# Moving work between engines and along the queues of two gated units: slope products, a normalisation and a gradient product

## The chip, the cores and the metric

The kernel runs on one core of one Trainium2 chip. Its time is the device time of a run in microseconds (us); a lower time is better. The time before is the median of six runs. All busy times, waits and durations come from one profiled execution of the kernel before. In the profile PE is TensorE (PEld its weight loads), DVE is VectorE, ACT is ScalarE, POOL is GpSimd, and SP is SyncE, which here only issues DMAs.

## The reference

Two kinds of layer alternate, A, B, A, B, over a residual x of 2048 rows and 512 columns, and the kernel returns the output and the gradients with respect to x and all weights.

```
def A(x): q, k, v = split(x @ wqkv)              # 32 heads of 16
          phi = t -> where(t > 0, t + 1, exp(t)) + 1e-6
          kv, z = phi(k)^T v, sum(phi(k));  return (phi(q) kv / (phi(q) z + 1e-6)) @ wo
def B(x): g = x @ w_gate;  u = x @ w_up;  h = sigmoid(g) * u;  return h @ w_down
x = x + A(layernorm(x));  x = x + B(layernorm(x))
x = x + A(layernorm(x));  x = x + B(layernorm(x))
out, vjp = jax.vjp(f, x, wqkv, wo, w_gate, w_up, w_down);  grads = vjp(grad_out)
```

The change lies in the two B layers, the gated units (GLU), with w_gate and w_up of 512 by 1376 and w_down of 1376 by 512. For the gradient a GLU needs, beside h, the two slopes: that of h with respect to u, which is sigmoid(g), and that with respect to g, which is sigmoid(g) (1 - sigmoid(g)) u.

## The kernel before, in words

The 2048 rows are 16 tiles of 128 and are worked on in 4 blocks of 4 tiles (512 rows). The 1376 inner columns of a GLU are 11 chunks of 128 (the last one overlaps its neighbour). Layers are numbered 0 to 3; 1 and 3 are the GLUs. The forward pass runs over the four layers, then the backward pass over layers 2, 1 and 0 (the backward products of layer 3 that lead to its input are made inside its forward loop), and the weight gradients come last.

**One chunk of a GLU** (`glu`). TensorE makes g (4 matmuls into one PSUM bank) and u (4 into another). ScalarE turns g in place into t = tanh(-g/2) (L647) and makes 1 - t in bf16 (L648). VectorE multiplies it by u/2: that is h (`hh`, L649). ScalarE makes 1 + t (L650), and GpSimd multiplies it by h (L651). So `sd` holds twice both slopes side by side. The forward pools have 8 PSUM banks, all under one tag, so a matmul group waits until an older bank has been read for the last time: u's by L649, g's by L650.

**The first GLU** (`b_fwd`, layer 1). For each block: the down product of the block before (44 matmuls into 4 banks, L675), its 4 residual adds on VectorE (`add_x`, L428), the normalisation of these 4 tiles for layer 2 (`nxt.need`), then the 11 chunks. The stores of a chunk's `hh` and `sd` (L657, L668) go to SP's queue one chunk later. Between the chunks the caller advances the second half of layer 0 by a step (`A0.second`): queries are evicted and scaled (L534, L535, L546), y products made and added, and these tiles normalised for layer 1. In the last block the keys of layer 2 are made between chunks 4, 6, 8 and 10.

**The normalisation** (`LN.one`, layers 1 to 3) takes two tiles at once: ScalarE makes the negative mean (L296) and twice the squared deviations with their sum (L299), GpSimd makes rstd (L301, L302), VectorE applies it (L304, two operations), and SP issues a transposing DMA (L307). After the fourth tile GpSimd's queue stores the block (L310).

**The last GLU** (`b_both`, layer 3). Per chunk it calls `glu`, then makes the gradient of h (4 matmuls), which ScalarE halves into `dhh` (L732, two buffers), and VectorE multiplies both slopes by it in place (L733): that is `dd`. SP stores it (block 0, L781) or transposes it into a staging tile (later blocks, L763), which is flushed at the second chunk of the next group. GpSimd's queue stores `hh`. After chunk 1 of a block come the down product of the block before (into the output, L718) and the 88 matmuls from its `dd` to the gradient of the normalised input (L790), with the backward normalisation (L855 to L862). Block 0 runs beside the second half of layer 2; when that is done, the transposed weights for the backward pass are loaded (L418, L419), held by `k.last_mul`, the last product L733 issued, and GpSimd clears their overlap (L420).

**What sets the order.** Each engine works its own queue in order. The order within a queue is set when the program is built, by the place in the code and a priority (`high_priority`), and it can differ from the order of the code; `after` pins some pairs by hand. Semaphores hold data dependences across engines.

Of the kernel before, what the change touches and what calls it, by code (L numbers as in the profile page):

```python
# [9 lines left out]
ACT = mybir.ActivationFunctionType  # L10
ALU = mybir.AluOpType
# [9 lines left out]
P = 128  # L21
NST = S // P
# [6 lines left out]
NB = 4  # L29
NBLK = NST // NB  # L30
SB = NB * P
# [7 lines left out]
def rows(st, n=1):  # L39
    return slice(st * P, (st + n) * P)  # L40


def by_tile(ap2d, st, n):
    return ap2d[rows(st, n), :].rearrange("(n p) d -> p n d", p=P)
# [133 lines left out]
def mm4(k, out, lhs, rhs, n=NDC):  # L178
    for c in range(n):
        i = k.nc.tensor.matmul(out, lhsT=lhs(c), rhs=rhs(c), start=(c == 0), stop=(c == n - 1))  # L180
    return i
# [153 lines left out]
def forward(k):  # L335
    nc, tc = k.nc, k.tc
    with ExitStack() as ctx:
# [22 lines left out]
        for b, fc in b_fwd(k, 1, lns[1], lns[2]):  # L360
            if fc < 7:
                next(second, None)
            if b == NBLK - 1 and fc in (4, 6, 8, 10):
                A2.keys((fc - 4) // 2)
# [58 lines left out]
def add_x(k, st, y_ps, x=None):  # L423

    if st % 2 == 0:
        k.sums[st // 2] = k.small.tile([P, 2], F32, name="x_sum", bufs=NST)
    t = k.sums[st // 2][:, st % 2:st % 2 + 1]
    k.nc.vector.scalar_tensor_tensor(k.xs[st][:], y_ps[:], 1.0, k.xs[st][:] if x is None else x, ALU.mult, ALU.add,  # L428
                                     accum_out=t)
# [202 lines left out]
                yield True  # L632


def glu(k, hT, fc):

    nc = k.nc
    g_ps = k.ps.tile([P, SB], F32, name="g_ps", tag="bank")
    mm4(k, g_ps[:], lambda c: k.wg[:, c, FC0[fc]:FC0[fc] + P], lambda c: hT[:, :, c, :])
    u_ps = k.ps.tile([P, SB], F32, name="u_ps", tag="bank")  # L640
    mm4(k, u_ps[:], lambda c: k.wu[:, c, FC0[fc]:FC0[fc] + P], lambda c: hT[:, :, c, :])
    hh = k.p_hh.tile([P, SB], BF16, name="hh_t")
    if k.n_sd % 2 == 0:
        k.sd2 = k.p_sd.tile([P, 2, 2, SB], BF16, name="sd_t", tag="sd")
    sd = k.sd2[:, k.n_sd % 2]
    k.n_sd += 1
    nc.scalar.activation(g_ps[:], g_ps[:], ACT.Tanh, scale=-0.5)  # L647
    nc.scalar.activation(sd[:, 0, :], g_ps[:], ACT.Identity, bias=k.onef[:], scale=-1.0)  # L648
    nc.vector.scalar_tensor_tensor(hh[:], sd[:, 0, :], 0.5, u_ps[:], ALU.mult, ALU.mult)  # L649
    nc.scalar.activation(sd[:, 1, :], g_ps[:], ACT.Identity, bias=k.onef[:])  # L650
    nc.gpsimd.tensor_tensor(sd[:, 1, :], sd[:, 1, :], hh[:], ALU.mult)  # L651
    return hh, sd


def store_hh(k, sv, b, fc, hh, eng):
    p0, f1 = (FDUP if fc == NFC - 1 else 0), min((fc + 1) * P, F)
    eng.dma_start(out=sv["hhT"][fc * P:f1, b * SB:(b + 1) * SB], in_=hh[p0:P])  # L657


def b_fwd(k, l, ln, nxt):  # L660
    nc, sv = k.nc, k.sv[l]
    hhs, late = {}, []

    def store():

        b, fc, hh, sd = late.pop()
        store_hh(k, sv, b, fc, hh, nc.sync)
        nc.sync.dma_start(out=sv["sd"][b, fc], in_=sd.rearrange("p a b -> p (a b)"))  # L668

    def down(b):  # L670
        ys = [k.ps.tile([P, D], F32, name="y_ps", tag="bank") for _ in range(NB)]
        for fcs in (range(NFC - 1), (NFC - 1,)):
            for j in range(NB):
                for fc in fcs:
                    nc.tensor.matmul(ys[j][:], lhsT=hhs[b][fc][:, rows(j)], rhs=k.wd[:, fc, :],  # L675
                                     start=(fc == 0), stop=(fc == NFC - 1))
        for j in range(NB):
            add_x(k, b * NB + j, ys[j])
        nxt.need(b * NB + NB - 1)

    for b in range(NBLK):
        hhs[b] = []
        if b:
            down(b - 1)
        for fc in range(NFC):
            hh, sd = glu(k, ln.hT[b], fc)
            hhs[b].append(hh)
            if late:
                store()
            late.append((b, fc, hh, sd))  # L690
            yield b, fc
    store()
    down(NBLK - 1)


def last_grads(k, b):

    k.gns[b] = k.p_h.tile([P, NB, D], BF16, name="gn_t", tag="h_t")
    k.nc.sync.dma_start(out=k.gns[b][:], in_=by_tile(k.g_in, b * NB, NB))
    k.gTs[b] = k.p_hT.tile([P, NDC, SB], BF16, name="gT3_t", tag="hT_t")  # L700
    k.nc.sync.dma_start_transpose(out=k.gTs[b][:], in_=k.g_in[rows(b * NB, NB), :])


def b_both(k, l, ln, ctx):

    nc, sv = k.nc, k.sv[l]
    pool = lambda name, bufs: ctx.enter_context(k.tc.tile_pool(name=name, bufs=bufs))
    hhs, dds, gns, gTs = {}, {}, k.gns, k.gTs
    k.n_t, k.fused = 2, lambda st: True

    def down(b):
        for j in range(NB):
            st = b * NB + j
            y_ps = k.ps.tile([P, D], F32, name="y_ps", tag="bank")
            mm4(k, y_ps[:], lambda fc: hhs[b][fc][:, rows(j)], lambda fc: k.wd[:, fc, :], NFC)
            if j % 2 == 0:
                ost = k.p_o.tile([P, 2, D], BF16, name="o0_t")
            nc.vector.tensor_tensor(ost[:, j % 2, :], y_ps[:], k.xs[st][:], ALU.add)  # L718
            if j % 2:
                k.st.dma_start(out=by_tile(k.out0, st - 1, 2), in_=ost[:])  # L720

    for b in range(NBLK):
        ln.need(b * NB + NB - 1)
        hhs[b], dds[b] = [], []
        if b == 1:
            k.p_ln, k.p_o, k.p_nat = pool("ln3", 2), pool("o3", 2), pool("nat", 2)
        for fc in range(NFC):
            hh, dd = glu(k, ln.hT[b], fc)
            ps = k.ps.tile([P, SB], F32, name="dhh_ps", tag="bank")
            mm4(k, ps[:], lambda c: k.wdT[:, c, FC0[fc]:FC0[fc] + P], lambda c: gTs[b][:, c, :])  # L730
            dhh = k.p_dhh.tile([P, SB], BF16, name="dhh_t")
            nc.scalar.mul(dhh[:], ps[:], 0.5)  # L732
            k.last_mul = nc.vector.tensor_tensor(dd, dhh[:].unsqueeze(1).to_broadcast([P, 2, SB]), dd, ALU.mult)  # L733
            hhs[b].append(hh)
            dds[b].append(dd)
            if b:
                turn_dd(k, sv, b, fc, dd)
            else:
                store_dd(k, sv, b, fc, dd, nc.sync)
            store_hh(k, sv, b, fc, hh, k.st)  # L740
            if fc == 1 and b:
                down(b - 1)
                dh_b(k, l, b - 1, dds[b - 1], ln.h[b - 1], gns[b - 1])
            if fc == 3 and b + 1 < NBLK:
                last_grads(k, b + 1)
                if b:
                    ln.need((b + 2) * NB - 1)
            if b == NBLK - 1 and fc == 5:
                k.early = a_grads(k, 0)
            yield b, fc  # L750
    b = NBLK - 1
    down(b)
    dh_b(k, l, b, dds[b], ln.h[b], gns[b])
    flush_nat(k)


def turn_dd(k, sv, b, fc, dd):

    i, f = divmod(fc, 4)
    p0 = FDUP if fc == NFC - 1 else 0  # L760
    if f == 0:
        k.nat = k.p_nat.tile([P, 2, NB, D], BF16, name="nat_t")
    k.nc.sync.dma_start_transpose(  # L763
        out=k.nat[:, :, :, f * P - p0:(f + 1) * P - p0].rearrange("p a j f -> p (a j) f"),
        in_=dd.rearrange("p a s -> p (a s)"))
    if f == 1:
        flush_nat(k)
    if f == 3 or fc == NFC - 1:
        w = SETS[i][1]
        k.nats.append((sv["ddN"][b, i, :, :, :, 0:w], k.nat[:, :, :, 0:w]))  # L770


def flush_nat(k):
    while k.nats:
        dst, t = k.nats.pop()
        k.nc.sync.dma_start(out=dst, in_=t)


def store_dd(k, sv, b, fc, dd, eng):
    p0, f1 = (FDUP if fc == NFC - 1 else 0), min((fc + 1) * P, F)  # L780
    eng.dma_start(out=sv["ddT"][:, fc * P:f1, b * SB:(b + 1) * SB].rearrange("a p s -> p a s"), in_=dd[p0:P])  # L781


def dh_b(k, l, b, dds, h, up=None):
    for j in range(NB):
        st = b * NB + j
        dh_ps = k.ps.tile([P, D], F32, name="dh_ps", tag="bank")
        for i in range(2 * NFC):
            a, fc = divmod(i, NFC)
            k.nc.tensor.matmul(dh_ps[:], lhsT=dds[fc][:, a, rows(j)], rhs=(k.wuT, k.wgT)[a][:, fc, :],  # L790
                               start=(i == 0), stop=(i == 2 * NFC - 1))
        ln_bwd(k, l, st, dh_ps[:], h[:, j, :], k.xs[st][:] if up is None else up[:, j, :])
# [462 lines left out]
```

## Time and profile before

| what | value |
|---|---|
| runs before, median (lowest to highest) | 1134.0 us (1131.3 to 1139.45) |
| profiled execution: run, span | 1132.12 us, 1130.3 us |
| granted TensorE clock | 0.995 of full speed |
| first GLU, from its first to its last matmul | 77.2 to 213.7 us |
| last GLU | 267.5 to 523 us |
| ScalarE busy in the chunks of block 1 of the first GLU (110.5 to 136.0) | 23.07 of 25.5 us |
| VectorE, GpSimd busy in the same stretch | 18.18, 15.65 us |
| TensorE busy in block 0 of the last GLU (267 to 324) | 48.49 of 57 us |
| L648, L650 on ScalarE, mean of one | 690 ns, 688 ns |
| L647, L732 on ScalarE, median of one | 593 ns, 597 ns |
| matmul of 512 columns, median record | 379 ns |

A group's line reads: line, engine, operation, output and inputs, shape, count, busy time and mean of one, then the engine's idle time just before these instructions and what ended most of it. In the timeline a row is start, duration, engine, line, operation, and in brackets the idle time before it and its releaser; xN says how many instructions are merged. In the waits a row is the waiting instruction, what it waited for, total time, how often, and the longest.

### The profile page before, as it was taken

The numbers are of one execution on the slowest core, as the hardware profiler recorded it, in microseconds if no ns is written. First come the engines' busy times: TensorE is split into PE (matmuls) and PEld (weight loads), VectorE is DVE, ScalarE is ACT, GpSimd is POOL, SyncE is SP. The second block draws the span as 40 slices with busy tenths as digits, with TensorE's granted clock in tenths as the row PEclk, the third lists the DMA queues.
The fourth block names the chain that finished last, engine by engine and source line by source line (L and its number), as shares of the span: only waits on it lengthen the run. The fifth ranks groups of instructions, "written<-read, shape, count | busy, mean of one in ns | idle before, by whom it ended". The sixth has DMA issues, their size and how long they took to land.

```text
span 1130.3 us, 15573 instructions
## 1 busy us (share of the span) xinstructions
PE 1073.6 (95%) x5529; PEld 508.8 (45%) x5624; DVE 527.5 (47%) x983; ACT 487.8 (43%) x1002; POOL 327.0 (29%) x427
## 2 busy tenths in 40 slices
PE   6989999998889999999998999999899999999998
PEld 3444444444344444444443444444444444465443
DVE  7685655667734445434756624556666200000100
ACT  3476977547635556453433533335336200000011
POOL 5425755303632526141533200003523100001110
PEclk9999999999999999999999999999999999999999
DMA  9987988679994939399995798759972797699995
GB/s 263 263 230 241 255 242 248 187 181 236 291 228 88 255 78 248 77 259 269 235 336 154 218 273 231 241 171 301 317 233 81 172 280 172 146 185 253 274 234 133
DMA packets 376557, 248.12 MB, mean 220 GB/s; under 512 B 288784, under 2 KB 341040, under 8 KB 374688
## 3 DMA queue, kind: packets, MB, share of 16 engines
q1 hardware_dynamic: 361424, 197.73, 70.1%
q0 software_dynamic: 15056, 49.39, 12.8%
q8 instruction: 44, 0.72, 0.3%
q14 instruction: 33, 0.27, 0.1%
HBM read 74.48 MB, written 102.20 MB: 156 GB/s over the span
## 4 chain that ended last, share of the span: by engine, by line
PE 27%; issue 20%; POOL 3%; DMA 3%; DVE 2%; ACT 1%; SPq 0%; POOLq 0%; DVEq 0%; ACTq 0%
PE dh_ps L885 7%; PE dhh_ps L180 3%; PE fill_ps L236 3%; PE dw_ps L1199 2%; PE CT_ps L972 2%; PE dq_ps L180 2%; PE dh_ps L790 2%; PE dh_ps L1107 2%; PE dh_ps L1046 1%; DMA qr_l<-sv_qr 1%; POOL out_dram L1127 1%; PE dpk_ps L180 1%; POOL x L865 1%; PE y_ps L180 1%; DMA hf_t<-sv_hhT 1%
## 5 line engine op out<-in xcount | busy, mean ns | idle before, releaser
L1199 PE MATMUL dw_ps<-set_t,h_all 128*128 128x512 bf16 (+1 forms) x1008 | 203.9, 362 | 2.3 <-ACT dw_new L1126 1.5
L1199 PEld LDWEIGHTS <-h_all 128*128 128x128 bf16 x1024 | 100.0, 98 | 105.6 <-issue 2.1
L651 POOL TENSOR_TENSOR sd_t<-sd_t,hh_t 128x512 bf16<-128x512 bf16 x88 | 107.8, 1235 | 119.8 <-DVE hh_t L649 89.2
L1126 ACT CAST dw_new<-dw_ps 128x512 bf16<-128x512 f32 (+1 forms) x40 | 19.9, 572 | 219.0 <-PE dw_ps L1199 155.2
L855 ACT ACTIVATE t_sb<-dh_ps,rstd 128x512 f32<-128x512 f32 x64 | 43.5, 680 | 134.1 <-PE dh_ps L790 81.6
L180 PE MATMUL g_ps<-hT_t,wg 128*128 128x512 bf16 x352 | 90.5, 379 | 7.3 <-DVE hh_t L649 4.0
L1223 DVE TENSOR_TENSOR dw_new<-dw_ps,part_l 128x512 bf16<-128x512 f32 (+1 forms) x11 | 7.3, 687 | 179.7 <-PE dw_ps L1217 166.2
L180 PE MATMUL u_ps<-hT_t,wu 128*128 128x512 bf16 x352 | 90.5, 379 | 0.6 <-DVE hh_t L649 0.6
L180 PE MATMUL dhh_ps<-gT_t,wdT 128*128 128x512 bf16 x341 | 89.3, 379 | 0.5
L649 DVE SCALAR_TENSOR_TENSOR hh_t<-sd_t,u_ps 128x512 bf16<-128x512 bf16 x88 | 59.3, 679 | 14.1 <-ACT sd_t L648 13.5
L885 PE MATMUL dh_ps<-wuT,dd_t 128*128 128x512 bf16 x173 | 65.6, 379 | 0.2
L885 PE MATMUL dh_ps<-wgT,dd_t 128*128 128x512 bf16 x170 | 64.5, 379 | 0.2
L1127 POOL DMA_DIRECT2D out_dram<-dw_new x36 | 19.2, 541 | 151.1 <-ACT dw_new L1126 149.6
L648 ACT ACTIVATE sd_t<-g_ps,onef 128x512 bf16<-128x512 f32 x88 | 60.8, 690 | 2.5
L650 ACT ACTIVATE sd_t<-g_ps,onef 128x512 bf16<-128x512 f32 x88 | 60.6, 688 | 0.0
L733 DVE TENSOR_TENSOR sd_t<-dhh_t,sd_t 128x1024 bf16<-128x1024 bf16 x44 | 30.4, 692 | 61.5 <-POOL sd_t L651 60.2
L908 DVE TENSOR_TENSOR dd_t<-dhh_t,sh_t 128x1024 bf16<-128x1024 bf16 x44 | 29.9, 689 | 58.6 <-ACT dhh_t L906 45.0
L647 ACT ACTIVATE g_ps<-g_ps 128x512 f32<-128x512 f32 x88 | 52.4, 602 | 8.8 <-PE g_ps L180 8.7
L180 PEld LDWEIGHTS <-wg 128*128 128x128 bf16 x352 | 33.9, 98 | 47.1 <-issue 8.8
L180 PEld LDWEIGHTS <-wu 128*128 128x128 bf16 x352 | 34.4, 98 | 42.4 <-issue 0.9
L790 PEld LDWEIGHTS <-sd_t 128*128 128x128 bf16 x352 | 34.4, 98 | 41.6
L885 PEld LDWEIGHTS <-dd_t 128*128 128x128 bf16 x352 | 34.4, 98 | 41.6
(172 smaller groups left out, 1854.7 us busy)
## 6 DMA issues: line engine op xcount, KB each, us to landing
sv_sd<-sd_t SPq DMA_DIRECT2D x44, 256.0 KB, 2.9
sv_ddT<-dd_t SPq DMA_DIRECT2D x40, 256.0 KB, 4.2
sv_h<-h_t POOLq DMA_DIRECT2D x16, 512.0 KB, 5.6
sv_qr<-pe_t POOLq DMA_DIRECT2D x16, 512.0 KB, 5.2
qr_l<-sv_qr SPq DMA_DIRECT2D x8, 1024.0 KB, 7.4
sh_t<-sv_sd SPq DMA_DIRECT2D x8, 1024.0 KB, 7.1
h_all<-sv_h SPq DMA_DIRECT2D x16, 512.0 KB, 5.8
sv_ddN<-nat_t SPq DMA_DIRECT2D x6, 1024.0 KB, 4.4
```

The costliest lines, as they stand in the source:

```text
L180: i = k.nc.tensor.matmul(out, lhsT=lhs(c), rhs=rhs(c), start=(c == 0), stop=(c == n - 1))
L236: nc.tensor.matmul(ps[0:w, :], lhsT=t[:, st, 0:w], rhs=self.g[st // NB][:, st % NB, :], start=(st == 0), stop=(st == NST - 1))
L647: nc.scalar.activation(g_ps[:], g_ps[:], ACT.Tanh, scale=-0.5)
L648: nc.scalar.activation(sd[:, 0, :], g_ps[:], ACT.Identity, bias=k.onef[:], scale=-1.0)
L649: nc.vector.scalar_tensor_tensor(hh[:], sd[:, 0, :], 0.5, u_ps[:], ALU.mult, ALU.mult)
L650: nc.scalar.activation(sd[:, 1, :], g_ps[:], ACT.Identity, bias=k.onef[:])
L651: nc.gpsimd.tensor_tensor(sd[:, 1, :], sd[:, 1, :], hh[:], ALU.mult)
L790: k.nc.tensor.matmul(dh_ps[:], lhsT=dds[fc][:, a, rows(j)], rhs=(k.wuT, k.wgT)[a][:, fc, :], start=(i == 0), stop=(i == 2 * NFC - 1))
L855: nc.scalar.activation(t_sb[:], dh_ps, ACT.Identity, scale=rstd, accum_out=c1[:])
L885: nc.tensor.matmul(acc[b][j][:], lhsT=dd[:, a, rows(j)], rhs=(k.wuT, k.wgT)[a][:, fc, :], start=(fc == 0 and a == 0), stop=(fc == NFC - 1 ...
L1127: (eng or k.st).dma_start(out=k.outs[nm][rs, cs], in_=new[0:r, 0:w])
L1199: k.nc.tensor.matmul(ps[ic][:, 0:w], lhsT=h_m[:, ic * P:(ic + 1) * P], rhs=t_m, start=(m == 0), stop=(m == n - 1))
```

## The change

`glu` gets a flag `fused`. With it, the second slope is made by one VectorE operation, (t + 1) times h, which reads t from PSUM, instead of the ScalarE and the GpSimd operation. The first GLU sets it in its odd chunks (1, 3, 5, 7, 9); the last GLU does not. In the first GLU the normalisation of the block before moves from its place after the residual adds to two places behind chunks 2 and 4, two tiles each; the last block's stays behind its adds. In the last GLU the product L733, and with it the store or transposes of `dd`, is issued one chunk later, behind the `dhh` of the next chunk; the last chunk's follows the loop.

```
-def glu(k, hT, fc):
+def glu(k, hT, fc, fused=False):
...
-    nc.scalar.activation(sd[:, 1, :], g_ps[:], ACT.Identity, bias=k.onef[:])
-    nc.gpsimd.tensor_tensor(sd[:, 1, :], sd[:, 1, :], hh[:], ALU.mult)
+    if fused:
+        nc.vector.scalar_tensor_tensor(sd[:, 1, :], g_ps[:], 1.0, hh[:], ALU.add, ALU.mult)
+    else:
+        nc.scalar.activation(sd[:, 1, :], g_ps[:], ACT.Identity, bias=k.onef[:])
+        nc.gpsimd.tensor_tensor(sd[:, 1, :], sd[:, 1, :], hh[:], ALU.mult)
...
         for j in range(NB):
             add_x(k, b * NB + j, ys[j])
-        nxt.need(b * NB + NB - 1)
...
         for fc in range(NFC):
-            hh, sd = glu(k, ln.hT[b], fc)
+            hh, sd = glu(k, ln.hT[b], fc, fc % 2 == 1)
...
             late.append((b, fc, hh, sd))
+            if b and fc in (2, 4):
+                nxt.need((b - 1) * NB + (1 if fc == 2 else 3))
             yield b, fc
     store()
     down(NBLK - 1)
+    nxt.need(NST - 1)
...
+    def scale(b, fc, dhh, dd):
+        k.last_mul = nc.vector.tensor_tensor(dd, dhh[:].unsqueeze(1).to_broadcast([P, 2, SB]), dd, ALU.mult)
+        if b:
+            turn_dd(k, sv, b, fc, dd)
+        else:
+            store_dd(k, sv, b, fc, dd, nc.sync)
+
+    late = []
...
             nc.scalar.mul(dhh[:], ps[:], 0.5)
-            k.last_mul = nc.vector.tensor_tensor(dd, dhh[:].unsqueeze(1).to_broadcast([P, 2, SB]), dd, ALU.mult)
+            if late:
+                scale(*late.pop())
+            late.append((b, fc, dhh, dd))
             hhs[b].append(hh)
             dds[b].append(dd)
-            if b:
-                turn_dd(k, sv, b, fc, dd)
-            else:
-                store_dd(k, sv, b, fc, dd, nc.sync)
...
+    scale(*late.pop())
     b = NBLK - 1
     down(b)
```

## The prediction

> **What bounds the kernel now.** I read the page first, then TensorE's waits over both gated units, then busy times by stretch, then the timeline around each stall. All times are us of the profiled execution: span 1130.3, run 1132.12, so 1.82 lies around the span; the median of the runs is 1134.0, 1.88 above that run. I sum against the profiled run and add the saving or loss to the median.
>
> From the page, engines and costliest groups:
>
> ```profile
> PE 1073.6 (95%) x5529; PEld 508.8 (45%) x5624; DVE 527.5 (47%) x983; ACT 487.8 (43%) x1002; POOL 327.0 (29%) x427
> ...
> L651 POOL TENSOR_TENSOR sd_t<-sd_t,hh_t 128x512 bf16<-128x512 bf16 x88 | 107.8, 1235 | 119.8 <-DVE hh_t L649 89.2
> ...
> L649 DVE SCALAR_TENSOR_TENSOR hh_t<-sd_t,u_ps 128x512 bf16<-128x512 bf16 x88 | 59.3, 679 | 14.1 <-ACT sd_t L648 13.5
> ...
> L733 DVE TENSOR_TENSOR sd_t<-dhh_t,sd_t 128x1024 bf16<-128x1024 bf16 x44 | 30.4, 692 | 61.5 <-POOL sd_t L651 60.2
> ```
>
> TensorE is the bound: nothing that only lightens another engine counts unless a TensorE gap closes. L733 shows 60.2 of VectorE idle behind GpSimd, but idle time on an engine that is not the bound is not yet a gain. So, TensorE's own waits between 77 and 523 (first GLU 77 to 214, last GLU from 267):
>
> ```profile
> PE y_ps L180 <- DVE pe_t L535: 5.3, 4, 2.6
> PE g_ps L180 <- DVE hh_t L649: 4.0, 5, 1.3
> PE y_ps L180 <- DVE hh_t L649: 2.9, 1, 2.9
> ...
> PE g_ps L180 <- ACT sd_t L650: 0.8, 1, 0.8
> ```
>
> Nearly all are waits for VectorE: PSUM banks that L649 has not yet freed, or queries that L535 has not yet scaled. By the timeline the first GLU has five: 1.31 at 116.42, 0.31, 0.21, 1.31 at 151.97, 1.00, together 4.14. The last GLU has eight that the change can reach: 0.40, 0.83, 1.33, 2.62 at 304.12, 2.90 at 324.46, 0.58, 0.73, 0.36, together 9.75. A stall costs a little more than the idle shown: four matmuls start 0.865 apart (110.60, 111.46), 0.216 each, but a record lasts 0.379, so 0.163 of each gap is covered by a modelled end. That gives 4.14 + 5 x 0.163 = 4.95 and 9.75 + 8 x 0.163 = 11.05. **The ceiling is 16.0.**
>
> **Part 1, the fused slope.** In 20 chunks (5 odd ones in each of 4 blocks) it removes an L650 (start to start 0.57 in an unbroken run) from ScalarE and an L651 (1.15) from GpSimd, and adds one VectorE operation with one PSUM and one SBUF input, 128x512 to bf16. The nearest row is L649, same shape: 0.68 alone, 0.63 start to start. Per block: ScalarE -2.85, GpSimd -5.75, VectorE +3.15. It waits for nothing new (it follows L649, whose result it reads, and the tanh is older), but it now frees the g bank, 0.63 after u's. Queued behind it: the next L649, adds, normalisations.
>
> **Part 2, the norm.** Its instructions stay the same and move from the block's head to after chunks 2 and 4, a pair of tiles each. On ScalarE a pair is about 1.6 start to start (0.17 + 2 x 0.71). Its transposes move past three chunks' stores in SP's queue, its store (0.82) past GpSimd's L651s. Cost nil: the turned tiles are first read by the keys in block 3, and the stored chunks' buffers return after 14 chunks. If the cover were gone, the next attention would open with the wait of such a transpose, 4.7 (its median from issue to landing). On VectorE, L304 waits for rstd, and the adds, L649 and fused products wait behind it.
>
> Do both fit? Blocks 0 and 3 have no gap. Block 1 before:
>
> ```profile
> 114.77 1.00 DVE L304 TENSOR_SCALAR h_t<-x,ln_neg,rstd 128x512 bf16<-128x512 f32 x2 [2.08 <-POOL rstd L302]
> ...
> 116.42 1.02 PE L180 MATMUL g_ps<-hT_t,wg 128*128 128x512 bf16 x4 [1.31 <-DVE hh_t L649]
> 116.76 1.15 POOL L651 TENSOR_TENSOR sd_t<-sd_t,hh_t 128x512 bf16<-128x512 bf16 x1
> 116.83 1.82 DVE L304 TENSOR_SCALAR h_t<-x,ln_neg,rstd 128x512 bf16<-128x512 f32 x2 [0.46 <-POOL rstd L302]
> ```
>
> The lump of four tiles stands before chunk 0's L649 while four y banks have only just come free; moving it removes this stall's cause. *ScalarE*: it ends L648 of chunk 9 at 137.7. Without 5 x 0.57 that is 134.9, and L649 makes hh at 135.6. TensorE, without its stalls, would start the down product at 136.14 - 1.31 - 0.31 - 0.33 = 134.2 and need hh of chunk 9 nine matmuls later, 136.1: it fits by 0.5. *VectorE*: from 110.15 until chunk 9's hh at 138.5 it passed 28.4, of which 7.3 idle, 6.7 of that at L304 (2.08, 0.46, 2.40, 1.77), so 21.1 busy. New: 24.2 of work in 136.1 - 110.15 = 25.95, so only 1.75 of idle is allowed; about 3.4 if the two L304 pairs that were stretched to 1.82 (see below) run at 1.00. So the idle at L304 has to halve. I expect that, since the 2.08 came from the lump and a fuller queue arrives later, but not wholly: in block 1 the pair after chunk 4 meets another norm from the attention's outputs, in block 2 four pairs follow each other. I take half: **2.5 of 4.95 come back**. Bounds: gain 4.95; or a loss of 12.6 if all 20 products land on the path.
>
> **Part 3, the product one chunk later.** Count and cost of L733 stay; only its place on VectorE moves behind the next chunk's L649. What it removes is a ring, seen in block 1 of the last GLU:
>
> ```profile
> 370.19 1.14 POOL L651 TENSOR_TENSOR sd_t<-sd_t,hh_t 128x512 bf16<-128x512 bf16 x1 [0.95 <-ACT dhh_t L732]
> ...
> 371.37 0.69 DVE L733 TENSOR_TENSOR sd_t<-dhh_t,sd_t 128x1024 bf16<-128x1024 bf16 x1 [1.32 <-POOL sd_t L651]
> ...
> 371.98 0.68 DVE L649 SCALAR_TENSOR_TENSOR hh_t<-sd_t,u_ps 128x512 bf16<-128x512 bf16 x1
> ...
> 372.82 1.14 POOL L651 TENSOR_TENSOR sd_t<-sd_t,hh_t 128x512 bf16<-128x512 bf16 x1 [0.94 <-ACT dhh_t L732]
> ```
>
> L733, L649, L651 and back take 2.62 a turn; TensorE needs 12 x 0.216 = 2.59 for a chunk. The ring is as slow as TensorE, so lateness is never made up. Afterwards VectorE needs 0.61 + 0.68 and ScalarE 0.6 + 0.57 + 0.57 + 0.6 = 2.3: slack appears. Worth, stall by stall: blocks 1 to 3 lose 0.58 + 0.73 + 0.36 + 0.49 = 2.2; at 275.04 a whole product leaves the front (0.56); at 291.34 a wait of 1.04 before L535 goes; at 304.12 two such waits, 2.0. At 324.46 GpSimd is held for 7.7 in a memset that waits for a weight load, and VectorE 8.3 behind it; with a chunk of slack, chunk 10's hh is done before the wait, and y's first bank is free: about 2.4 of 3.06. The 0.83 waits for ScalarE and stays. Sum 8.2. In block 0 ScalarE (four rd evictions together, norm pairs) is next late, so I take 0.6 of it: **5.0**. Bounds: 0 and 11.
>
> Every DMA after the product (the transposes of dd, block 0's stores of it, on SP) moves one chunk, 2.6; the one of chunk 1 moves behind 29 of down and dh products, with the flush of the staging tile. Their readers come in the end stage; dh reads dd 11 chunks later, and the last product is issued before the last down product (9.5). dhh has two buffers: L732 of chunk c+2 waits for L733 of c, now after L649 of c+1, still earlier than ScalarE's third operation of c+2. Cost nil; with that cover gone, 0.6 a chunk.
>
> A rule speaks against part 3. Before, L733 never ran beside L651, since it waited for it; now both start after L649.
>
> ```profile
> 300.51 1.22 DVE L546 SCALAR_TENSOR_TENSOR pe_t<-pe_t,rd_t 128x1024 bf16<-128x1024 bf16 x1
> ...
> 300.73 2.00 POOL L651 TENSOR_TENSOR sd_t<-sd_t,hh_t 128x512 bf16<-128x512 bf16 x1 [1.44 <-issue]
> ```
>
> Here L651 takes 2.00 instead of 1.14 beside a VectorE operation on two SBUF tensors, and at 116.83 L304 loses 0.82 to an L651 that started 0.07 earlier. The Trainium skill ("SBUF — State Buffer", "Who interferes with whom" and "SBUF: two separate sides") says VectorE's second SBUF port is GpSimd's and is locked for a whole instruction: who comes first goes, the other stands. L733 has two SBUF inputs. If GpSimd always came first, VectorE would stand 1.15 again and part 3 gain nothing. By the rows L651 starts 0.16 after L649 ends while VectorE's next operation follows at once, so GpSimd loses about 0.6: its chunk is then 1.15 + 0.6 + 0.58 (the hh store) = 2.3, under 2.59. I go by the rows. The fused slope has one SBUF input and takes no lock; L649 beside L651 leaves it at 1.15.
>
> **Sum.** 2.5 + 5.0 = 7.5: 1132.1 - 7.5 = 1124.6 on the profiled run, 1134.0 - 7.5 = **1126.5** as a median.
>
> **Rivals.**
> *VectorE becomes the first GLU's bound (slower).* Place: L304 and what queues behind it. For: 24.2 of work in 25.95. Against: ScalarE gets lighter and half of the L651s that blocked L304 go. It decides once VectorE's idle at L304 stays near 6.7 a block: all 12.6 of fused products then land on TensorE's path and nothing of the 4.95 returns; less 5.0 from part 3, +7.6: 1141.6.
> *The gaps only move.* The queues are not in program order in the trace (L546 of slope(2,0) runs before an earlier chunk's L649), so the product may not stand where the code puts it; or ScalarE is next. For: TensorE is 95% busy. Within 4 either way: about 1133.
> *All gaps close.* 16.0: 1118.0. Against: the 0.83 and part of 2.62 have other causes.
>
> **Chances.** Forecast, gain 4 to 12: 0.55. Gaps only move: 0.28. Slower: 0.12. All close: 0.05. A difference of 0.5%, 5.7, is about what a measurement can tell from none. Faster by more: 0.45 of the forecast's share and the 0.05, 0.50; slower by more: 0.11; same: the rest, 0.39. The forecast's own range is 1122 to 1130; leaving out the slow case and the far end (0.17), the range is 1120.5 to 1137.
>
> **What would show it.** Right: L733 no longer idle behind L651 (60.2 to under 15); no TensorE gap over 0.5 after 325; the gaps at 116 and 152 gone; L650 and L651 at 68. Part 1 wrong: new TensorE waits on L649 or on the fused line before 214, with L304's idle not fallen. Part 3 wrong: L733 at 1.3 or more beside L651, or ScalarE waiting at L732. I am wrong in sum if the other queues give the gaps back before 523.

## The result, and the profile after

The changed kernel took 1128.71 us (median of 15 runs, 1124.46 to 1131.8) against 1133.2 for the kernel before beside it (34 runs). The two medians lie 4.5 apart; the recorded ratio of the runs is 0.9954, 95% interval 0.9935 to 0.9972, which is 5.2 us less (3.2 to 7.4). The forecast was 7.5. The profiled execution ran 1127.75 us, with a span of 1126.0.

Some lines moved: L650 is now L653 (ScalarE), L651 the new VectorE slope and L654 the GpSimd slope, L733 is L728, L732 is L745, L675 is L678, L790 is L802. From the page after, engines and groups:

```profile
PE 1073.1 (95%) x5529; PEld 509.4 (45%) x5624; DVE 536.5 (48%) x1003; ACT 477.1 (42%) x982; POOL 303.2 (27%) x407
...
L654 POOL TENSOR_TENSOR sd_t<-sd_t,hh_t 128x512 bf16<-128x512 bf16 x68 | 83.6, 1230 | 153.6 <-DVE hh_t L649 108.4
...
L649 DVE SCALAR_TENSOR_TENSOR hh_t<-sd_t,u_ps 128x512 bf16<-128x512 bf16 x88 | 59.5, 679 | 10.5 <-ACT sd_t L648 9.8
...
L728 DVE TENSOR_TENSOR sd_t<-dhh_t,sd_t 128x1024 bf16<-128x1024 bf16 x44 | 30.4, 691 | 60.9 <-POOL sd_t L654 59.5
```

ScalarE is 10.7 lighter and GpSimd 23.8, about as worked out (20 x 0.57 and 20 x 1.15). The surprise is the last line: the product still stands 59.5 behind the GpSimd slope, where it should have been under 15. TensorE's waits over both GLUs (77 to 524):

```profile
PE y_ps L180 <- DVE pe_t L535: 3.1, 4, 1.9
...
PE dh_ps L802 <- DMA wgT<-in_B_w_gate_dram: 1.8, 1, 1.8
PE y_ps L678 <- DVE hh_t L649: 1.7, 3, 0.8
...
PE g_ps L180 <- DVE hh_t L649: 1.1, 2, 0.7
PE fill_ps L236 <- ACT t_sb L867: 0.9, 1, 0.9
PE g_ps L180 <- ACT sd_t L653: 0.8, 1, 0.8
PE u_ps L180 <- DVE hh_t L649: 0.6, 1, 0.6
```

The waits at g for L649 fell from 4.0 to 1.1 and the 2.9 at y is gone. Two kinds are new or have grown: the down product of the first GLU waits for L649 (1.7, and 0.2 before), and a weight load is late (1.8).

To see where a kernel gains, I cut each trace at three of TensorE's matmuls: the first of the first GLU, the first of the last GLU, and the first filler of the backward pass (L236, at 523.61 before). The last column is from there to the end.

| kernel | first GLU to last GLU | last GLU to filler | filler to end | ratio of times, 95% interval |
|---|---|---|---|---|
| before | 190.26 | 256.11 | 606.7 | |
| before, profiled again | 190.25 | 255.93 | 610.4 | |
| changed | 188.26 | 252.36 | 608.5 | 0.9954 (0.9935 to 0.9972) |
| first GLU's part only | 188.28 | 253.60 | 608.8 | 0.9973 (0.9955 to 0.9991) |
| last GLU's part only | 190.54 | 251.16 | 608.9 | 0.9970 (0.9954 to 0.9986) |
| load order only | 190.24 | 254.67 | 609.2 | 0.9986 (0.9969 to 1.0004) |
| fused slope only | 189.85 | 254.80 | 606.0 | 0.9958 (0.9940 to 0.9976) |
| fused slope only, again | 189.84 | 253.83 | 610.1 | 0.9980 (0.9964 to 0.9997) |
| norm spread only | 193.00 | 254.58 | 607.3 | 1.0017 (1.0003 to 1.0031) |
| changed, product pinned | 188.28 | 248.32 | 612.2 | 0.9923 (0.9894 to 0.9952) |
| changed, product pinned, again | 188.28 | 247.57 | 612.6 | 0.9926 (0.9901 to 0.9950) |
| pinned, fused in the last GLU too | 188.27 | 251.50 | 611.6 | 0.9922 (0.9900 to 0.9944) |
| pinned and fused, no norm spread | 189.84 | 247.88 | 610.1 | 0.9924 (0.9898 to 0.9949) |
| product pinned, nothing else | 190.27 | 248.41 | 599.8 | 0.9913 (0.9882 to 0.9944) |

So the changed kernel gained 2.0 in the first GLU and 3.8 in the last one. Every kernel with the moved product, pinned or not, also has the other load order that comes with it (below). The last column scatters by 4 for one and the same program (606.7 and 610.4; 606.0 and 610.1), so a single trace's span says little. In the three programs traced twice the first column repeats within 0.02 and the second within 1.0. Below, "saved up to the filler" compares the sum of the first two columns with the mean of the two traces of before, 446.3.

The last GLU's column holds a scatter of its own. One part is the stall at 324.46: 2.90 and 2.38 in the two traces of before, and 1.57 (norm spread only), 1.00 (fused slope only, again), 0.41 (first GLU's part only) and none (fused slope only) in four traces whose last GLU is the same. It grows with the time for which GpSimd's two memsets wait for their weight loads (7.70 + 0.76 before, 7.16 + 0.78 in its repeat, 5.74 + 0.81 where it is 1.00). The other part is the clock: in the trace without the stall (254.80) TensorE was granted 0.50 for 3.4 us from 303.4 on. So six traces of one and the same last GLU reach from 253.6 to 256.1, and the 3.8 of the changed kernel is measured from their upper end.

### The profile page after: what moved, and what is told of

It reads as the page before. It is cut to its first block, busy times and chain, and to the rows that moved or that the text cites. A ratio compares the mean times of both kernels' runs of the same rounds, so it can differ in the third digit from the quotient of the medians.

```text
span 1126.0 us, 15526 instructions
## 1 busy us (share of the span) xinstructions
PE 1073.1 (95%) x5529; PEld 509.4 (45%) x5624; DVE 536.5 (48%) x1003; ACT 477.1 (42%) x982; POOL 303.2 (27%) x407
## 4 chain that ended last, share of the span: by engine, by line
PE 26%; issue 21%; POOL 3%; DMA 3%; DVE 2%; ACT 1%; SPq 0%; POOLq 0%; DVEq 0%; ACTq 0%
PE dh_ps L897 7%; PE dhh_ps L180 3%; PE fill_ps L236 3%; PE dw_ps L1211 2%; PE CT_ps L984 2%; PE dq_ps L180 2%; PE dh_ps L802 2%; PE dh_ps L1119 2%; DMA qr_l<-sv_qr 2%; PE dh_ps L1058 2%; POOL out_dram L1139 1%; PE dpk_ps L180 1%; POOL x L877 1%; PE y_ps L180 1%; DMA pkT_l<-sv_pkT 1%
## 5 line engine op out<-in xcount | busy, mean ns | idle before, releaser
L654 POOL TENSOR_TENSOR sd_t<-sd_t,hh_t 128x512 bf16<-128x512 bf16 x68 | 83.6, 1230 | 153.6 <-DVE hh_t L649 108.4
L649 DVE SCALAR_TENSOR_TENSOR hh_t<-sd_t,u_ps 128x512 bf16<-128x512 bf16 x88 | 59.5, 679 | 10.5 <-ACT sd_t L648 9.8
L648 ACT ACTIVATE sd_t<-g_ps,onef 128x512 bf16<-128x512 f32 x88 | 60.4, 689 | 2.8
L728 DVE TENSOR_TENSOR sd_t<-dhh_t,sd_t 128x1024 bf16<-128x1024 bf16 x44 | 30.4, 691 | 60.9 <-POOL sd_t L654 59.5
L802 PEld LDWEIGHTS <-sd_t 128*128 128x128 bf16 x352 | 34.4, 98 | 43.5 <-issue 2.0
L180 PEld LDWEIGHTS <-wdT 128*128 128x128 bf16 x352 | 34.4, 98 | 41.4
```

## The experiments

**One part at a time.** The changed file with the old `b_both`, and the old file with the new one.

```
-            hh, sd = glu(k, ln.hT[b], fc)
+            hh, sd = glu(k, ln.hT[b], fc, fc % 2 == 1)
...
+            if b and fc in (2, 4):
+                nxt.need((b - 1) * NB + (1 if fc == 2 else 3))
```

> Only the first GLU's part of the change (fused slopes and spread norm); the last GLU as before. Theory A (both parts act: about 2.0 us in the first GLU, about 3.5 us in block 0 of the last GLU): the last GLU starts 2.0 us earlier than before, its own length is as before (256.1 us from its first matmul to 523.6), time about 2 us under before, ratio 0.998. Rival B (only the first GLU's part works, the last GLU only runs differently because its start moved): about 5 us under before, ratio 0.9955, as the whole change.

```
+            if late:
+                scale(*late.pop())
+            late.append((b, fc, dhh, dd))
```

> Only the last GLU's part. Theory A: first GLU as before with its five gaps, last GLU 3.5 us shorter, time about 3 us under before, ratio 0.997. Rival B: no different from before, ratio 1.000. In both, VectorE's idle before the product stays near 60 us in blocks 1 to 3 of the last GLU, because its queue there still alternates L649 and the product of the same chunk.

Measured: the first part alone 0.9973, its stretch 188.28; the last part alone 0.9970, its stretch 251.16. Each saves in its own stretch (2.0, and 4.9) about what the changed kernel saves there (2.0 and 3.8; 1.2 of the difference is a weight load's wait of 0.56 in place of 1.76), so neither needs the other. The first part alone missed its expectation in one point: its last GLU, which is unchanged, took 253.60 and not 256.1, since the stall was 0.41 in this trace. Its ratio doesn't separate the two theories (0.9955 to 0.9991). In the last part alone the product still waits 57.8 for GpSimd and the gaps of 0.59, 0.74 and 0.35 on L649 stay: the ring is there without the first part as well.

**The product pinned.** The changed kernel, with an explicit order between the product of chunk c - 1 and the L649 of chunk c (left out at chunk 2 of the later blocks, where a down product lies between).

```
+    k.last_hh = nc.vector.scalar_tensor_tensor(hh[:], sd[:, 0, :], 0.5, u_ps[:], ALU.mult, ALU.mult)
...
                 scale(*late.pop())
+                if fc != 2 or b == 0:
+                    after(k, k.last_mul, k.last_hh)
```

> The change, with each product of the last GLU pinned behind the next chunk's L649 on VectorE (except over the down product), so that the product really stands one chunk later. If the ring of product, L649 and GpSimd's slope is what makes the gaps of 0.58, 0.73 and 0.35 in blocks 1 to 3 (my prediction's reason): these three gaps go, VectorE's idle before the product falls from 60 to under 20, and the time is 2 us under the changed kernel, ratio to before about 0.9935. Rival: the shared port makes product and slope stand for each other (slope 1.75 instead of 1.15, or product 1.3), ScalarE waits for dhh buffers, and the gaps stay: ratio 0.9955 as the change.

Measured: 0.9923; the last GLU 248.32, that is 4.0 less than in the changed kernel; the product's wait 12.5 and no gap on L649 left. Of the 4.0, 2.3 come from blocks 1 to 3, where the three gaps were, and 0.5 from the head of block 0; 1.2 is again a weight load's wait (0.60 in place of 1.76, and none in the repeat), which scatters. For the question whether the product stands where the source puts it, this is the decisive run. In the changed kernel VectorE's queue in blocks 1 to 3 has the very order of before, product of c - 1, then h of c; the source puts it one chunk later, the program as built does not. The changed kernel's timeline shows the ring unbroken:

```profile
365.60 0.69 DVE L728 TENSOR_TENSOR sd_t<-dhh_t,sd_t 128x1024 bf16<-128x1024 bf16 x1 [1.32 <-POOL sd_t L654]
366.21 0.68 DVE L649 SCALAR_TENSOR_TENSOR hh_t<-sd_t,u_ps 128x512 bf16<-128x512 bf16 x1
...
367.05 1.14 POOL L654 TENSOR_TENSOR sd_t<-sd_t,hh_t 128x512 bf16<-128x512 bf16 x1 [0.95 <-ACT dhh_t L745]
...
368.22 0.69 DVE L728 TENSOR_TENSOR sd_t<-dhh_t,sd_t 128x1024 bf16<-128x1024 bf16 x1 [1.33 <-POOL sd_t L654]
```

365.60 to 368.22 is 2.62 a turn, as before.

**The load order.** The change makes `k.last_mul`, which holds the backward weight loads, one product older, and with it the loads of one weight come together. The old kernel with only that:

```
-            k.last_mul = nc.vector.tensor_tensor(dd, dhh[:].unsqueeze(1).to_broadcast([P, 2, SB]), dd, ALU.mult)
+            k.last_mul, k.this_mul = getattr(k, "this_mul", None), nc.vector.tensor_tensor(dd, dhh[:].unsqueeze(1).to_broadcast([P, 2, SB]), dd, ALU.mult)
```

> The kernel before, with only the hold on the backward weights' loads one product older, as a side effect of the change made it; products stand where they stood. The loads then stand in SP's queue in the changed kernel's order (large, small, large, small) and the first memset behind the last chunk's slope. If the 2.90 us gap at the end of block 0 came from GpSimd's memset that stood ahead of two chunks' slopes: this gap goes, about 1.8 us comes back as a wait for the last weight load, and the time is 1 to 1.5 us under before, ratio 0.999. Rival (the product's place alone made block 0 shorter): gap as before, ratio 1.000.

Measured: 0.9986 (an interval that holds 1), last GLU 254.67. The stall of 2.90 at 324 goes, 1.33 and 2.62 before it stay. In the kernel before GpSimd's first memset stands ahead of two slopes that here run before it. The kernel before, then this one:

```profile
320.19 0.51 POOL L420 MEMSET wuT<- 32x512 bf16 x1 [7.70 <-DMA wuT<-in_B_w_up_dram]
...
321.95 1.14 POOL L651 TENSOR_TENSOR sd_t<-sd_t,hh_t 128x512 bf16<-128x512 bf16 x1
```

```profile
318.98 1.15 POOL L651 TENSOR_TENSOR sd_t<-sd_t,hh_t 128x512 bf16<-128x512 bf16 x1 [0.94 <-ACT dhh_t L732]
...
326.14 0.52 POOL L420 MEMSET wuT<- 32x512 bf16 x1 [5.50 <-DMA sv_ddT<-sd_t]
```

The 1.8 that I expected back as a wait for the last weight load did not come. That the trace saves 1.4, and not the 3.0 of the stall, has another reason: after the wait of 2.62 the clock was granted at half for 3.4 us, and in the kernel before, after the same wait, it was not. Windows over that stretch, here and in the kernel before (the clock is third from the end):

```profile
303.70:307.10 3.40, 3.11 (x8) 1.18 (x9) 3.19 (x7) 0.20 (x1) 0.90 (x3) 0.50 1.06 284
```

```profile
303.90:307.30 3.40, 3.18 (x15) 1.48 (x16) 3.40 (x8) 0.80 (x2) 0.91 (x3) 1.00 1.03 280
```

Seven matmuls fewer, at 0.216 each, are 1.5. So the load order takes away the stall, whatever its length; in the six traces of the old order that is 0 to 2.90, 1.4 in the mean. The times (1.6, from -0.5 to 3.5) don't tell it from nothing.

**The first GLU taken apart.** The old kernel with the fused slope alone, and with the spread alone.

```
-            hh, sd = glu(k, ln.hT[b], fc)
+            hh, sd = glu(k, ln.hT[b], fc, fc % 2 == 1)
```

> The kernel before with only the fused slope in the odd chunks of the first GLU; the normalisation stays in its lump at the block's head. With both parts the first GLU took 188.3 us from its first matmul to the last GLU's (190.3 before). Theory: the lump of four L304 at each block's head makes the two waits of 1.31 (at 116.42 and 151.97 before), and the fused slope only lightens ScalarE; so both waits of about 1.3 stay, at most the 1.00 at 154.85 shrinks, and the stretch is 189.5 to 190.5; time 0.999 to 1.001. Rival: the fused slope does the work, through ScalarE and through fewer GpSimd slopes that lock L304: stretch 188.0 to 188.8, the two waits under 0.8. Second rival: the added 3.15 us of VectorE work per block without the spread makes it worse: over 191.

```
-        nxt.need(b * NB + NB - 1)
...
+            if b and fc in (2, 4):
+                nxt.need((b - 1) * NB + (1 if fc == 2 else 3))
```

> The kernel before with only the spread of the normalisation in the first GLU (a pair of tiles after chunks 2 and 4), all 20 slopes left on ScalarE and GpSimd. Theory: the spread alone takes the two waits of 1.31 away, but ScalarE, with 2.85 us more per block than in the changed kernel, is then late for the down product: waits of 0.6 to 1.0 appear near 136 and 152, the stretch is 188.3 to 189.3, time 0.997 to 0.999. Rival (the slope does it): the stretch stays at 190.0 or more, with waits on L649 of over 1.2 at the blocks' heads.

Fused slope alone, TensorE's timeline: both waits of 1.31 stand as in the kernel before, and the stretch (189.85) is 0.4 shorter.

```profile
115.97 1.02 PE L180 MATMUL g_ps<-hT_t,wg 128*128 128x512 bf16 x4 [1.31 <-DVE hh_t L649]
151.19 1.02 PE L180 MATMUL g_ps<-hT_t,wg 128*128 128x512 bf16 x4 [1.31 <-DVE hh_t L649]
```

Spread alone, the same view: these two waits are gone, and later ones take more than their place.

```profile
130.24 1.02 PE L180 MATMUL g_ps<-hT_t,wg 128*128 128x512 bf16 x4 [1.07 <-DVE x L428]
...
140.07 0.39 PE L678 MATMUL y_ps<-wd,hh_t 128*128 128x512 bf16 x1 [2.16 <-DVE hh_t L649]
...
172.07 1.02 PE L180 MATMUL g_ps<-hT_t,wg 128*128 128x512 bf16 x4 [1.51 <-ACT sd_t L653]
```

The stretch is 193.00, which is 2.75 longer, and the kernel is slower (1.0017): I had expected 188.3 to 189.3. The direction of the theory was right, its size was not: ScalarE makes L648 late for the down product, but it had itself stood 3.15 before 134.28 for a residual add (L428), which VectorE did after an L304 that waited for GpSimd's rstd. So the lump makes the two waits, and the spread pays only beside the fused slope: 0.4 for the slope alone, -2.75 for the spread alone, 2.0 together. Whether the lighter ScalarE or the lighter GpSimd does it, these runs don't separate. The ratio of the fused slope alone (4.8 us) did not fit its trace (1.6 up to the filler), so it ran again:

> The fused slope alone again. Its trace saved 0.4 us in the first GLU and 1.3 in the last one, of which code and order are unchanged, against 4.8 us by its median (interval 2.7 to 6.8). Theory: the trace is right and the median was high by chance: 0.9970 to 0.9990. Rival: 0.9958 within 0.001 again, so that fewer slopes on GpSimd win something that one profile doesn't show.

It gave 0.9980, which is 2.3 us; its trace saved 2.6. The first ratio had most likely been high by chance.

**The pinned product alone, and pinned with the fused slope but no spread.** The same pin as above, in the changed kernel without the spread, and without both parts of the first GLU.

> The pinned kernel without the spread of the normalisation: fused slopes in the first GLU's odd chunks, the norm in its lump at the block's head, the product pinned one chunk later. By the traces the spread is worth 1.6 us on top of the fused slope (first GLU 189.85 with the slope alone, 188.3 with both): first GLU about 189.9, ratio 1.5 us above the pinned kernel's of the same call (0.9923 before): 0.993 to 0.995. Rival, by the medians (slope alone 0.9958, both 0.9973, spread alone 1.0017): the spread costs about 1.7 us somewhere, and this kernel is faster than the pinned one, 0.990 to 0.9915.

> The kernel before with the gradient product pinned one chunk later in the last GLU, and nothing else: the first GLU as before. Theory: the parts add; pinned and both parts gave 0.9923, the first GLU's part alone 0.9973, so 0.995, which is 5.7 us; last GLU to first filler 248 to 250.5 (256 before), product idle behind the GpSimd slope under 20 (60.2 before), no gaps on L649 in blocks 1 to 3. Rival: the pinned product gains only where GpSimd is lightened elsewhere or ScalarE has slack: 0.997 or more, with 253 or more.

Measured: 0.9924 and 0.9913, last GLU 247.88 and 248.41. The first has the first GLU that its theory said (189.84), but a ratio between the two theories: the spread's 1.6 of the trace shows in no ratio. The second did in the last GLU what its theory said, but is quicker than both expected (0.995, 0.997): the pinned product, with the load order that comes with it, is as quick as all together. So in time the parts don't add up as I had them; once the product is pinned, the first GLU's 2.0 can't be told from nothing (the ratios' intervals are some 0.5% wide). Tile `sd_t` in the last GLU of this smallest version, durations as minimum, median and longest, then the GpSimd wait:

```profile
L654 POOL TENSOR_TENSOR sd_t<-sd_t,hh_t x44: 1139/1456/3398, 270.9 to 486.8; 128x512 bf16<-128x512 bf16 x44
L726 DVE TENSOR_TENSOR sd_t<-dhh_t,sd_t x44: 677/684/2251, 275.9 to 488.3; 128x1024 bf16<-128x1024 bf16 x44
...
  POOL sd_t L654: 12.7, 7
```

And one turn of it:

```profile
371.73 0.69 DVE L649 SCALAR_TENSOR_TENSOR hh_t<-sd_t,u_ps 128x512 bf16<-128x512 bf16 x1 [1.03 <-ACT sd_t L648]
...
372.33 0.68 DVE L726 TENSOR_TENSOR sd_t<-dhh_t,sd_t 128x1024 bf16<-128x1024 bf16 x1
372.56 1.46 POOL L654 TENSOR_TENSOR sd_t<-sd_t,hh_t 128x512 bf16<-128x512 bf16 x1 [0.33 <-ACT sd_t L653]
...
374.00 0.69 DVE L649 SCALAR_TENSOR_TENSOR hh_t<-sd_t,u_ps 128x512 bf16<-128x512 bf16 x1 [0.98 <-ACT sd_t L648]
```

The product now stands behind h, its slope's wait is gone, and a turn takes 2.27 (371.73 to 374.00): VectorE waits for ScalarE's L648, whose four operations are 2.3. The ring was the limit, and ScalarE is the next one, under TensorE's 2.59.

**The fused slope in the last GLU too**, on the pinned kernel:

```
-            hh, dd = glu(k, ln.hT[b], fc)
+            hh, dd = glu(k, ln.hT[b], fc, fc % 2 == 1)
```

> The pinned kernel with, besides, the fused slope in the odd chunks of the last GLU too (ScalarE loses 20 L653, GpSimd 20 slopes there, VectorE gets 20 operations of about 0.63 us). Pinned, the last GLU took 248.3 us from its first matmul to the backward's first filler, the slope on GpSimd had a median of 1457 ns and single products lasted up to 2247 ns. Theory of the shared port: with half of the slopes gone, products of the fused chunks run beside nothing, the product's mean falls by 0.1 us or more and its longest stays below 2.3; TensorE has no gap left in blocks 1 to 3 to win, so what can be won is in block 0, where L535 and the slope of 2.00 stand against each other: 246 to 248.5, time 0.990 to 0.993. Rival: VectorE is block 0's bound (its queue feeds L535, L649 and the norm), and 3.15 us more of it cost up to as much: 249 to 251.5, time 0.994 to 0.996.

Measured: 0.9922, and the longest product is 693 ns (2247 pinned): with half of the GpSimd slopes gone no product is held any more. TensorE gains nothing from it, since it had no gap to lose in blocks 1 to 3: from its first matmul to the end of the last dh product it takes 247.7 (pinned 247.5 and 246.7). The 251.5, in the rival's range, comes from a wait of 3.85 behind that, for a load of the first filler, and not from VectorE as the rival had it; why this load is later here than elsewhere (0.87 to 1.70) is not shown.

**Repeats for the scatter.** The kernel before, and the pinned kernel, again.

> The kernel before, unchanged, profiled once more. From the first backward filler to the end it took 606.7 us in the first profile and 608.5 to 612.2 in the five other kernels, whose code is the same there. In the weight-gradient stage its wait for one set of turned factors was 2.6 us (near 1052) against 4.2 to 5.1 in the others. Theory: that wait is the scatter of a stretch in which the DMA engines are full (busy share 1.05 to 1.2), not the price of arriving earlier: here it reads anywhere from 2.6 to 5.2, and filler to end 606 to 610. Rival: the transfers have a floor in time, so whoever arrives earlier waits longer: again 2.6 within 0.5, and 606.7 within 0.5.

> The pinned kernel again, in one call with the two before, so that they compare directly. First GLU 188.3 and last GLU 248 to 249 again, within 0.5 and 1.5; ratio 0.9923 within 0.002. From first filler to end it took 612.1 us, although every engine has the same order there as in the kernel before. Theory of scatter: 606 to 612, most likely under 611. Rival, that the pinned product costs something at the end: 612 within 0.7.

The kernel before took 610.4 from filler to end, 3.7 more than in its first profile and 0.4 past what I had allowed; its wait for the turned factors was 2.8, close to the 2.6 of before, so that wait does not make the 3.7 (what does is in the last section). The pinned kernel gave 612.6 after 612.2, as the rival had it, while the pinned product alone gave 599.8 and the pinned kernel without the spread 610.1. All engines have the same order there in the kernel before, the changed one and the smallest pinned one. Whether the pinned kernel has a price of its own at the end stays open; its ratios (8.7 and 8.4 us less than before) leave room for 1 to 2 us of it, against the 9.7 and 10.4 that its traces save up to the filler.

## Why the prediction came out as it did

**The sum, 7.5.** 5.2 was measured: inside the forecast of 4 to 12, near its low end, and with an interval (3.2 to 7.4) that reaches into the rival "the gaps only move". The traces give 2.0 + 3.8 up to the filler. In part 3 it is near for a wrong reason.

**Part 1 and 2, 2.5 of 4.95: mechanism right in the main, size near.** 2.0 came back. The two gaps at 116 and 152 went, as said. The condition that the idle at L304 halve was nearly met: 19.1 over the four blocks before, 10.2 after. But it was the wrong gauge: with the fused slope alone it falls to 12.6 too, and both gaps stay. The budget said that chunk 9's h "fits by 0.5" for the down product; it missed, and what is late next is there, in the changed kernel's first GLU:

```profile
136.60 0.39 PE L678 MATMUL y_ps<-wd,hh_t 128*128 128x512 bf16 x1 [0.75 <-DVE hh_t L649]
137.66 7.73 PE L678 MATMUL y_ps<-wd,hh_t 128*128 128x512 bf16 x35 [0.68 <-DVE hh_t L649]
153.11 0.61 PE L180 MATMUL y_ps<-M_t,pe_t 128*128 128x512 bf16 x2 [0.57 <-DVE pe_t L535]
169.70 9.79 PE L678 MATMUL y_ps<-wd,hh_t 128*128 128x512 bf16 x43 [0.23 <-DVE hh_t L649]
```

The spread's "cost nil" holds only beside the fused slope: alone it costs 2.75. A cost of nil was argued from transposes and stores; ScalarE, which runs the norm's pairs of 1.6, was budgeted only with the fused slope's relief.

**Part 3, the step that failed: "its place on VectorE moves behind the next chunk's L649".** It did not, in blocks 1 to 3: the order is unchanged, the product's wait is 59.5, and 0.58, 0.73 and 0.35 stand where 0.58, 0.73 and 0.36 stood. The prediction had this as the reason behind a rival (the queues are not in program order) and gave it 0.28; it should have costed part 3 for the case that the order stays. The runs that pin the order show what the argument was worth. In the smallest pinned version, by how much earlier the same matmul starts than in the kernel before, counted from the last GLU's first matmul:

| stall before | forecast | saved when pinned |
|---|---|---|
| 0.40 at 275.04 | 0.56 | 0.57 |
| 0.83 (for ScalarE) | 0 | 0.4 |
| 1.33 at 291.34 and 2.62 at 304.12 | 3.0 | 1.8 |
| 2.90 at 324.46 | 2.4 | 3.1 |
| blocks 1 to 3 | 2.2 | 2.3 |
| together | 8.2 | 8.1 |

The stretch itself fell by 7.7, since the filler's wait at its end is 0.4 longer. So the ring was rightly read, block 0 was not (at 304.12 the wait fell only to 1.92, where 2.0 was to go), and the sum is right because errors cancel; the 3.1 is the stall that scatters in the unchanged code. The discount to 0.6, reasoned from ScalarE in block 0, was not needed; that it brought the forecast near 3.8 was chance.

**Where the 3.8 came from instead.** Block 0. There the order did change around L535: the waits fell from 1.33 to 0.24 and from 2.62 to 1.92, and TensorE came out of the two 2.2 earlier. The stall of 2.90 went (3.1), as it goes with the load order alone, and 1.9 came back at once as a wait of 1.76 in the changed kernel's timeline; the filler's wait is 0.4 shorter:

```profile
330.57 2.54 PE L802 MATMUL dh_ps<-wgT,sd_t 128*128 128x512 bf16 x10 [1.76 <-DMA wgT<-in_B_w_gate_dram]
```

Loading one weight whole before the other frees the down product and can delay the dh product: its wait is 1.76 here, 0.56 in the last part alone, and none with the load order alone. The prediction had listed SP's transposes as moved and at no cost; that the hold on the loads moves with the product was not seen.

**The lock.** "GpSimd loses about 0.6" was too much for the common case and too little for the rare one. In the turn above the product starts 0.23 ahead and the slope lasts 1.46 in place of 1.15, so it loses 0.31. In the rare one it is VectorE that loses: three of 44 products last 2.2 in place of 0.7, to the end of a whole slope and beyond, as in the smallest pinned version here:

```profile
365.14 0.58 POOL L660 DMA_DIRECT2D sv_hhT<-hh_t  x1
365.22 2.25 DVE L726 TENSOR_TENSOR sd_t<-dhh_t,sd_t 128x1024 bf16<-128x1024 bf16 x1 [0.44 <-POOL sd_t L654]
365.75 1.17 POOL L654 TENSOR_TENSOR sd_t<-sd_t,hh_t 128x512 bf16<-128x512 bf16 x1
```

This product started 0.53 ahead of the slope, so "who comes first goes", as the prediction had it, does not cover it. All three start about 0.1 after GpSimd's issue of a DMA and 0.5 ahead of a slope; products that start as soon after an issue, but with no slope behind them (380.93, 437.34), last 0.69. What happens there stays open. Neither loss cost a TensorE gap in blocks 1 to 3.

**The rest of the kernel.** I let a gain before 523 pass to the end undiminished. By the times of the runs it does: in eleven of the twelve kernels with a ratio the trace's saving up to the filler lies within the interval of the time saved (changed kernel 5.7 against 3.2 to 7.4; the first run of the fused slope alone does not). Single traces don't show it, for a reason told below.

## What to carry to other kernels

A line moved in the source is a wish; before pricing a move, ask what decides the queue's order when the program is built, and pin the pair if the gain hangs on it: here the pin took 4.0 more from the last GLU, where the move alone had taken 3.8. A lump that is spread needs slack on every engine that its parts cross (alone it cost 2.75 here), so take the parts of a change alone and together. And list what hangs on the moved instruction besides its data: a hold that names "the last product" moves with it.

## What the runs showed of the hardware

**A short wait can cost twice.** In the weight gradients TensorE waits once for turned factors. In the changed kernel it waits 4.16 there. The windows from 1044.9, columns as in the profile with the granted clock third from the end:

```profile
1044.90:1049.00 4.10, 0.00 (x0) 0.00 (x0) 2.66 (x4) 0.00 (x0) 2.16 (x4) 0.80 1.18 294
1049.00:1054.00 5.00, 4.97 (x12) 2.00 (x13) 0.00 (x0) 0.00 (x0) 0.00 (x0) 0.50 1.16 306
```

For 5 us after the wait the clock is granted at half, and only 12 matmul records start in place of 24. In the smallest pinned version the same wait is 2.21:

```profile
1040.00:1042.30 2.30, 0.09 (x2) 0.03 (x2) 2.00 (x4) 0.00 (x0) 1.63 (x4) 1.00 1.24 279
1042.30:1047.30 5.00, 5.00 (x24) 2.44 (x24) 0.00 (x0) 0.00 (x0) 0.53 (x1) 1.00 1.13 262
```

No loss at all. In the kernel before, the same wait is 2.64 and the clock is 0.69 over the next 5 us; but the wait of 2.90 at 324.46 is followed by full clock, and one wait of 2.62 at 304 by full clock in the kernel before and by half with the load order alone. The Trainium skill ("TensorE: Matmul & The Clock Gate", "What's actually happening") has the halved clock follow an idle window of about 3.4 us that runs freely. The half agrees. The length does not: waits of 2.62 and 2.64 were enough here, though one of 2.90 was not.

It explains most of the scatter from filler to end. The kernel before (606.7) has three stretches at 0.50 there, 3.4 us each (from 596.6, 808.2 and 1054.0), which at half speed lose about 5.1; the smallest pinned version (599.8) has none. That is 5.1 of the 6.9 between them. The repeat of the kernel before (610.4) has 17.0 us at 0.50 (6.8 from 596.0, 6.8 from 797.4, 3.4 from 1056.8), which lose 8.5: 3.4 of the 3.7 by which it is longer.

**GpSimd can starve.** One slope of the smallest pinned version lasted 3.40 beside three VectorE operations in a row, as it did in all four traces of the pinned product without fused slopes in the last GLU:

```profile
286.75 0.69 DVE L535 TENSOR_TENSOR pe_t<-pe_t,rd_t 128x1024 bf16<-128x1024 bf16 x1
286.78 3.40 POOL L654 TENSOR_TENSOR sd_t<-sd_t,hh_t 128x512 bf16<-128x512 bf16 x1
287.35 1.22 DVE L546 SCALAR_TENSOR_TENSOR pe_t<-pe_t,rd_t 128x1024 bf16<-128x1024 bf16 x1
...
288.48 0.69 DVE L535 TENSOR_TENSOR pe_t<-pe_t,rd_t 128x1024 bf16<-128x1024 bf16 x1
```

It started 0.03 after the first of them and ended at 290.18, 1.0 after the third's end at 289.17, which is about its own length. The rows fit a slope that stands until all three have passed.
